# A recurrence feeding two gated layers: in the last two batches the r·u·k sums come from natural rows on GpSimd and VectorE instead of from one-column products

## The chip, the cores and the metric

The kernel runs on one core of one Trainium2 chip. The metric is device time in microseconds (us) for one execution: 479.68 us, the median of 3 runs (478.99 to 479.83). The engines are named as the profile names them: PE is TensorE (PEld its weight loads), DVE is VectorE, ACT is ScalarE, POOL is GpSimd, and SP issues the transfers.

## The reference

```python
B, H, S, D = 4, 8, 768, 48
for t in range(S):                                     # attention
    cur = einsum('bhd,bhe->bhde', u[None] * k_t, v_t)
    y[:, :, t] = einsum('bhd,bhde->bhe', r_t, state + cur)
    state = w_t[..., None] * state + einsum('bhd,bhe->bhde', k_t, v_t)
x = y.transpose(0, 2, 1, 3).reshape(B, S, H * D)       # 384 wide
h = gelu_tanh(x @ w_in);  u, v = h[..., :512], h[..., 512:]     # first layer
v_n = (v - mean(v)) / sqrt(var(v) + 1e-6) * g_ln
v_s = einsum('ts,bsd->btd', w_sg, v_n) + b_sg
x = x + (u * v_s) @ w_out                              # w_out 512 x 384
gate = sigmoid(causal convolution of x with 5 taps)    # second layer
out = (gate * (x @ w_val)) @ w_o2
```

The part that the change concerns is the own-token term of the recurrence: `r_t · (u * k_t)` is one number per token and head, the sum over d of r·u·k, and it scales v_t. Call these numbers the sums of r·u·k: 8 heads by 768 tokens in each of 4 batches.

## The kernel before

**The attention in units.** The recurrence is done in chunks of 64 tokens. A *unit* is one batch, one segment of 256 tokens and one pair of heads, so there are 12 units in a batch (3 segments by 4 pairs) and 48 in all. One packed transfer, `pk`, brings w, k and r of a unit with channels on the partitions; `sv` brings v for the chunks, and `v` (tile `vt`) brings natural rows of v: tokens on the partitions, all 384 columns.

A unit goes through these steps, whose letters the code uses. F and E (lines 396 and 401) are scans on DVE that make products of decays; L (`r_part`, 405) multiplies r by E on POOL; K (`k_part`) multiplies k by F; q (`ruk`, 412) multiplies r by k into the tile `q`. On PE, t (`turn`) transposes the decayed k; s (`scores`) makes the chunk's scores; B (`kv`, 447) makes each chunk's sum of k times v, and then the sums of r·u·k; C (`tokens`, 500) makes the outputs. After t, ACT copies the transposes (`kx`); after s, DVE masks the scores (`mx`). After B, ACT starts the chunk states (`gx`) and DVE chains them (step a, `states`, 491: tile `st`), then z saves the carry. `own_v` (o, 462) has ACT copy the sums out of PSUM (tile `rsw`) and POOL multiply natural v by them into the tile `y`. `y_out` (y, 515) adds what C made to `y`.

**The sums of r·u·k before.** In `kv`, lines 456 to 460, eight products of a unit take a 64 x 64 block of q as weights and one column of u (in the tile `misc`) as the moving operand: `pe.matmul(out=o[hh][half[c2], RS + j:RS + j + 1], lhsT=q[half[hh], ...], rhs=u_col[half[hh], ...])`. Each is a *one-column product*. A float32 product on 64 x 64 blocks stands in the trace as two records, so a unit has 16 of them.

**Visits.** All PE work of a unit's neighbours shares one two-bank PSUM tile, `p`. A *visit* is C of unit n-2, B of unit n-1, and t and s of unit n (`VISIT`, line 537). The results must be read out before the next visit writes there.

**The dense work.** Everything else on PE is dense: `xT` turns y, `hv` and `ups` are the two halves of x @ w_in, `vps` mixes tokens with w_sg, `c` is the first output product, `val` and `o` belong to the second layer. Weights and activations are split in high and low parts, so that each product takes three passes. The attention of batch b + 1 runs beside the dense work of batch b (`phase`, line 830); the last batch's dense work runs alone.

**What sets the order.** The program first records every instruction under a word with a number (`kx3`, `vs17`), and then emits them in the order of the list `SCHEDULE` (lines 55 to 193, used at 934). Each engine takes its own instructions in that order, one queue per engine; the transfers stand in SP's queue in the same way.

Of the kernel before, what the change touches and what calls it, by code (L numbers as in the profile page):

```python
# [15 lines left out]
F32 = mybir.dt.float32  # L16
# [7 lines left out]
DM = H * D  # L24
# [31 lines left out]
ini0 pk0 zp0 wps0 ld1 pk1 sv9 pk2 wl0 nat0 ld0 F0 wl1 sv2 K0 E0 wl2 sv0 F1 L0 pk3 E1 wm0 wm4 F2 L1  # L56
t0 wm4 wl3 q1 s0 K1 wm1 kx1 q0 dec0 wm2 wl4 K2 t1 sv3 dec0 s1 wm3 E2 sg0 kx0 dec1 dec0 B0 sv6 L2 mx1
mx0 dec0 ox0 wm9 ow0 gx2 wm9 wm10 pk4 dec1 gx1 kx2 wm10 dec0 sv1 ow2 t2 gx0 wm5 dec1 ow3 wm6 dec2 q2
pk5 B1 a0 dec1 wm7 dec2 s2 a0 dec3 wl5 F3 C0 kx3 dec2 kx4 E3 dec4 dec2 L3 gx4 ox1 gx3 z0 ox2 mx2 yc1
gx5 dec3 ow1 K3 wm15 ow7 yx0 wm15 dec3 B2 dec4 wm8 pk10 dec3 pk6 wm16 a1 dec4 sv4 wm11 a1 sg1 q3  # L60
dec3 pk9 C1 nat1 dec1 spl9 sv11 wm12 F4 spl0 yc0 wm16 spl9 t3 s3 dec4 dec5 wm13 dec2 gx6 wm14 gx7
ow5 wm17 E4 kx5 wm18 gx8 spl1 dec5 L4 z1 mx3 ox3 yx1 ow8 wm21 dec4 yd0 yc2 wm21 spl4 wm22 dec5 wm19
wl6 ow9 K4 ow6 mx5 sg2 ow4 mx4 B3 spl2 dec5 pk7 spl3 pk8 a2 wm22 spl1 spl10 wl7 sv7 a2 C2 ow10 F5
wl8 s4 sv10 t4 K5 z2 yx2 wm20 pk11 gx9 dec5 U4 wm27 yc3 wm27 ox4 ox5 wm23 gx11 spl10 gx10 wl9 wm28
ow13 wm24 kx6 a3 ow11 q4 ow15 E5 kx7 B4 spl5 spl2 dec6 L5 wm28 spl11 mx6 t5 yx4 wm25 yx3 a3 yd1 dec6
s5 C3 q5 spl0 wm29 ox6 yc4 ow12 wm29 spl11 yd2 wm30 gx12 ow16 wm30 ow14 F6 wm26 spl3 gx14 nat2 U5
gx13 sv5 dec7 yx5 xT0 a4 ow18 yc5 xTo0 dec7 yd3 xT1 a4 spl5 z3 xTo0 hv0 xTo1 mx7 kx8 dec7 K6 hv0 sg5
xTo1 dec6 hv0 a4 E6 hv1 ln0 F7 L6 C4 z4 dec6 B5 K7 s6 mx8 t6 E7 wm31 yc6 gx17 hv1 gx16 q6 U7 L7 yc7
ln0 kx9 wm31 mx10 hv1 ow17 dec7 gx15 U6 wm32 a5 kx10 dec7 ox7 ow19 B6 ox8 a5 ow23 q7 ln1 wm32 a5 F8
C5 s7 K8 yx7 yx6 t7 mx9 E8 yd4 wm33 gx18 gx19 wm33 wm34 kx11 z5 a6 ln0 gx20 wm34 a6 ow22 B7 ow21 L8  # L70
a6 ox9 ow20 spl8 t8 spl4 yx8 U8 s8 ln1 mx11 ow26 C6 z6 ow27 F9 ln1 sg4 gx22 sv8 gx21 kx12 a7 yc9 sg3
yc8 E9 gx23 wm35 yd5 kx13 ow25 a7 wm35 ox11 wm36 K9 ow24 q8 ow29 wm36 ox10 ln1 L9 t9 mx12 B8 yx10
ow31 a7 spl7 C7 dec6 pk12 ow28 s9 F10 ow30 gx24 yc10 ln0 K10 yx9 yx11 wm37 E10 ox12 spl6 xT2 wm37
wm38 ln0 xTo2 L10 wm38 ow34 xTo2 hv2 gx25 kx14 a8 U10 spl8 mx14 hv2 mx13 gx26 z7 ow32 a8 hv2 yd6 U9
a8 yc11 ow35 F11 yd7 wm39 ln2 t10 q9 B9 E11 s10 C8 q11 pk13 L11 sv13 xT3 ow33 ln2 q10 kx16 K11 wm39
gx29 wm40 yx13 gx27 gx28 wm40 a9 ox14 ln2 yc12 t11 xTo3 mx15 a9 spl7 kx15 xTo3 ox13 ow39 B10 ow38
yx12 mx16 ln2 s11 a9 C9 q12 U11 F12 hv3 ox15 gx30 ow42 a10 yc13 kx17 wm41 q13 gx31 wm41 K12 yc14
wm42 gx32 a10 wm42 ow37 E12 ow40 B11 ow43 a10 ow36 L12 mx17 C10 F13 yd8 hv3 pk14 ox17 gx33 ow45 nat3
gx34 a11 hv3 ox16 ow41 K13 ld2 ow44 a11 yc16 E13 gx35 yc15 ln3 a11 L13 yx16 yx15 yx14 t12 ln2 pk15
wm43 yd9 wm43 ln1 s12 yd10 ow47 C11 kx18 ln3 F14 spl6 yc17 kx19 ow46 spl13 yx17 xT4 spl13 s13 yd11  # L80
xTo4 B12 mx19 spl12 ln3 xTo4 xT5 E14 t13 xTo5 hv4 spl12 L14 dec9 mx18 hv4 gx36 xTo5 gx37 dec8 a12
hv5 dec9 gx38 q15 ln3 hv4 dec8 dec9 kx20 a12 hv5 dec9 ln4 K14 u0 z12 dec8 hv5 dec9 dec8 wl10 u0 ox18
ln5 ln3 sv12 o12 u0 mx20 u1 dec8 B13 ln4 F15 wl11 ln4 dec10 vs0 spl15 dec10 q14 t14 ln4 dec10 C12
K15 pk16 dec10 spl14 spl15 s14 wl12 uo0 vs0 E15 wl13 gx39 nat4 u1 ln4 L15 sv14 vs0 mx21 dec11 yx18
vs1 dec10 dec11 kx21 u1 spl14 gx40 vs1 dec11 uo1 a13 dec11 vs0 gx41 ox19 yc18 a13 vs2 dec11 yd12 vs1
cw0 ln5 F16 dec12 ln5 vs1 spl16 z13 dec12 C13 ln5 spl16 B14 dec12 dec13 ln5 vs0 dec13 vs1 dec12
dec13 s15 dec12 t15 dec13 vs0 E16 vs1 vs2 dec13 L16 vso0 vs2 spl18 wl14 vso1 vs2 ix2 gx43 wl15 kx22
wl16 spl17 vs2 gate0 sv15 gx44 ix1 gate1 vs2 gate0 pk17 mx22 gate1 gate0 ix0 yc19 gx42 gate1 u2 vso2
dec14 o13 wo0 K16 u2 dec14 spl17 u3 a14 vs3 dec15 dec14 a14 ox20 u2 spl18 o14 yx19 vs3 dec16 dec15
yd13 U16 z14 dec16 B15 dec14 s16 dec16 C14 dec14 vs3 dec15 spl19 dec16 t16 spl19 vs3 gx47 yc20 dec16  # L90
ox21 vs3 sg6 F17 spl21 vs3 gx46 u3 uo2 q16 gx45 spl21 wo1 pk18 dec15 wo2 sv16 a15 sg9 u3 i0 K17
# [922 lines left out]
```

## Time and profile before

| | |
|---|---|
| median of 3 runs | 479.68 us |
| the profiled execution | 479.42 us, of which the span of the trace is 477.5 us |
| PE busy | 456.3 us, 96% |
| DVE busy | 390.9 us, 82% |
| ACT busy | 266.5 us, 56% |
| POOL busy | 141.8 us, 30% |
| transfers | 44.03 MB, mean 92 GB/s |

An engine's share of the span is a mean over stages that differ, so it is read stage by stage. Matmuls are pipelined and their ends are modelled; two neighbouring rows of a PE timeline can overlap, and what a group of matmuls costs PE is the distance from its start to the start of the next group.

### The profile page before, as it was taken

The numbers are of one execution on the slowest core, as the hardware profiler recorded it, in microseconds if no ns is written. First come the engines' busy times: TensorE is split into PE (matmuls) and PEld (weight loads), VectorE is DVE, ScalarE is ACT, GpSimd is POOL, SyncE is SP. The second block draws the span as 40 slices with busy tenths as digits, with TensorE's granted clock in tenths as the row PEclk, the third lists the DMA queues.
The fourth block names the chain that finished last, engine by engine and source line by source line (L and its number), as shares of the span: only waits on it lengthen the run. The fifth ranks groups of instructions, "written<-read, shape, count | busy, mean of one in ns | idle before, by whom it ended". The sixth has DMA issues, their size and how long they took to land.

```text
span 477.5 us, 14571 instructions
## 1 busy us (share of the span) xinstructions
PE 456.3 (96%) x5940; PEld 412.0 (86%) x5940; DVE 390.9 (82%) x956; ACT 266.5 (56%) x810; POOL 141.8 (30%) x209
## 2 busy tenths in 40 slices
PE   8877898999999999999999999999999999999996
PEld 4655676888989988999999988999999989999995
DVE  5999999999998788767999899677988894326783
ACT  1586998744745388523745398433534696224253
POOL 4227655343523322322126122330133313100200
PEclk9899999999999999999999999999999999999999
DMA  8986124644413411143134131133122100000002
GB/s 265 353 265 207 27 71 134 185 142 127 134 44 88 140 55 47 47 131 108 44 93 135 45 101 60 35 101 113 39 77 85 35 1 1 34 18 0 1 17 83
DMA packets 25218, 44.03 MB, mean 92 GB/s; under 512 B 2880, under 2 KB 16832, under 8 KB 25152
## 3 DMA queue, kind: packets, MB, share of 16 engines
q1 hardware_dynamic: 25152, 43.11, 28.7%
q8 instruction: 46, 0.75, 0.7%
q14 instruction: 20, 0.16, 0.1%
HBM read 38.39 MB, written 4.72 MB: 90 GB/s over the span
## 4 chain that ended last, share of the span: by engine, by line
PE 71%; DVE 12%; ACT 5%; DMA 3%; issue 2%; POOL 1%; SPq 1%; ACTq 0%
PE vps L939 18%; PE p L939 11%; PE c L939 9%; PE ups L939 8%; PE hv L939 8%; PE o L939 8%; PE val L939 7%; DVE spare L939 3%; ACT vg L939 1%; DMA bits<-in_w_o_dram 1%; DMA bits<-in_w_val_dram 1%; DVE st L939 1%; PE a L939 1%; DVE F L939 1%; DVE late L939 1%
## 5 line engine op out<-in xcount | busy, mean ns | idle before, releaser
L939 PE MATMUL vps<-wsg,vnt 128*128 128x384 f32 x576 | 116.7, 341 | 0.0
L939 PEld LDWEIGHTS vps<-wsg,vnt 128*128 128x128 f32 x576 | 99.9, 188 | 0.6
L939 PE MATMUL ups<-x,win 128*128 128x384 f32 x288 | 61.9, 342 | 1.7 <-DVE gl L939 1.1
L939 PE MATMUL c<-gl,late 128*128 128x384 f32 x288 | 60.4, 340 | 0.0
L939 PE MATMUL hv<-win,x 128*128 128x512 f32 x216 | 58.2, 404 | 0.9 <-DVE x L939 0.9
L939 POOL TENSOR_TENSOR L<-pk,E 128x256 f32<-128x256 f32 x38 | 27.4, 722 | 98.4 <-PE p L939 29.9
L939 ACT ACTIVATE st<-p,F 128x48 f32<-128x48 f32 x144 | 39.9, 305 | 24.7 <-PE p L939 23.8
L939 PEld LDWEIGHTS ups<-x,win 128*128 128x128 f32 x288 | 50.6, 188 | 3.2 <-DVE gl L939 1.4
L939 PEld LDWEIGHTS c<-gl,late 128*128 128x128 f32 x288 | 50.0, 188 | 1.4 <-DVE gl L939 0.3
L939 DVE SCALAR_TENSOR_TENSOR cvp<-x,cw_col,cvp 128x384 f32<-128x384 f32 x84 | 49.7, 615 | 1.1 <-ACT cvp L939 0.5
L939 DVE SCALAR_TENSOR_TENSOR st<-st,F 128x48 f32<-128x48 f32 x128 | 40.8, 319 | 11.2 <-ACT st L939 10.3
L939 PE MATMUL o<-late,ml 128*128 128x384 f32 x216 | 47.1, 345 | 0.0
L939 PEld LDWEIGHTS hv<-win,x 128*128 128x128 f32 x216 | 38.8, 189 | 8.8 <-DVE x L939 1.7
L939 PE MATMUL val<-x2hl,late 128*128 128x384 f32 x216 | 43.7, 340 | 0.7 <-DVE gl L939 0.6
L939 POOL TENSOR_TENSOR x<-x 128x384 f32<-128x384 f32 x24 | 25.9, 1091 | 46.4 <-DVE cvp L939 43.5
L939 PEld LDWEIGHTS o<-late,ml 128*128 128x128 f32 x216 | 37.8, 188 | 2.1 <-DVE ml L939 0.7
L939 PEld LDWEIGHTS val<-x2hl,late 128*128 128x128 f32 x216 | 37.6, 188 | 1.9 <-DVE gl L939 0.9
L939 POOL TENSOR_TENSOR y<-s,y 128x96 f32<-128x96 f32 x48 | 24.8, 520 | 47.7 <-ACT s L939 17.7
L939 DVE TENSOR_TENSOR_SCAN F<-pk,D1F 128x260 f32<-128x260 f32 x40 | 29.9, 748 | 4.0 <-DMA pk<-in_pk_dram 3.7
L939 POOL TENSOR_TENSOR y<-v,rsw 128x192 f32<-128x192 f32 x36 | 20.6, 573 | 42.0 <-ACT rsw L939 30.6
L939 PEld LDWEIGHTS <-D1F 128*128 128x128 bf16 x196 | 18.6, 104 | 15.6 <-issue 8.1
L939 DVE SCALAR_TENSOR_TENSOR vps<-vps,misc,b_bc 128x384 f32<-128x384 f32 x29 | 17.9, 620 | 16.9 <-PE vps L939 16.9
(129 smaller groups left out, 935.1 us busy)
## 6 DMA issues: line engine op xcount, KB each, us to landing
pk<-in_pk_dram SPq DMA_DIRECT2D x40, 386.5 KB, 3.3
v<-in_v_dram SPq DMA_DIRECT2D x12, 384.0 KB, 4.2
out_dram<-ot SPq DMA_DIRECT2D x24, 192.0 KB, 2.1
sv<-in_sv_dram SPq DMA_DIRECT2D x39, 96.0 KB, 3.1
bits<-in_w_in_dram SPq DMA_DIRECT2D x6, 512.0 KB, 7.4
room_l<-in_pk_dram SPq DMA_DIRECT2D x7, 386.5 KB, 6.3
bits<-in_w_o_dram SPq DMA_DIRECT2D x7, 384.0 KB, 5.6
spare<-in_w_sgT_dram SPq DMA_DIRECT2D x12, 192.0 KB, 2.8
```

The source lines that it names most:

```text
L939: f(*a, **k)
```

## The change

For the units of batches 2 and 3 (the third and the fourth), step q, the one-column products and `own_v` are left out. In their place comes `bonus`, once for each 128 tokens, 6 times a batch and 12 times in all. A transfer `rk` brings natural rows of r and k (128 tokens by twice 384 columns, 384 KB) into one buffer; POOL multiplies r by k, then by u (a tile `u_bc`, loaded once, with u on every partition); DVE sums each head's 48 columns (`tensor_reduce`, 384 columns to 8); POOL multiplies natural v by these sums into `y`. The next `rk` load must wait for the reduce, since there is one buffer. Batches 0 and 1 keep the one-column products; the tile that held q in three slots becomes the `rk` buffer, and batch 1 keeps its q there. A visit is recorded with s before t, and the whole list `SCHEDULE` is another one, 2846 entries in place of 2860, from the first load to the last store.

```diff
 SCHEDULE = """
-ini0 pk0 zp0 wps0 ld1 pk1 sv9 pk2 wl0 nat0 ld0 F0 wl1 sv2 K0 E0 wl2 sv0 F1 L0 pk3 E1 wm0 wm4 F2 L1
...
+gate18 u20 yx45 bon11 gate18 u20 gx122 gate19 mx48 wo55 uo20 a40 ix12 gate19 wo54 K42 wo56 L42 vs20
...
+    u_bc = const.tile([128, DM], F32, name="u_bc")
...
-             "D1E": (NW, 1, ""), "st": (SV, 3, ""), "cy": (D, NP, ""), "q": (SEG, 3, "")}
+             "D1E": (NW, 1, ""), "st": (SV, 3, ""), "cy": (D, NP, ""), "rk": (2 * DM, 1, "")}
...
+    def load_rk(i):
+        t = buf("rk", i, i // KS).rearrange("p (two f) -> p two f", two=2)
+        with step("rk"):
+            sp.dma_start(out=t, in_=rk_[i // KS, i % KS * 128:(i % KS + 1) * 128, :, :])
+
+    def bonus(b, i):
+        s, j = divmod(i, NT)
+        with step("bon"):
+            t = buf("rk", b * KS + i, b)
+            q = t[:, 0:DM]
+            pool.tensor_tensor(out=q, in0=q, in1=t[:, DM:2 * DM], op=ALU.mult)
+            pool.tensor_tensor(out=q, in0=q, in1=u_bc, op=ALU.mult)
+            hd = lambda a: a.rearrange("p (h d) -> p h d", d=D)
+            rs = r2.tile([128, H], F32, tag="rsn", name="rs")
+            dve.tensor_reduce(out=rs, in_=hd(q), op=ALU.add, axis=AX.X)
+            run_loads("rk", b * KS + i + 1)
+            if j == 0:
+                yt[b, s] = ry.tile([128, NT, DM], F32, tag="y", name="y")
+            pool.tensor_tensor(out=hd(yt[b, s][:, j, :]), in0=hd(vt[b, s][:, j, :]),
+                               in1=rs.unsqueeze(2).to_broadcast([128, H, D]), op=ALU.mult)
+
...
-        q = pkt[:, 0:SEG] if first else parts["q"][1][n % 3]
+        q = pkt[:, 0:SEG] if first else parts["rk"][1][0][:, n % 3 * SEG:(n % 3 + 1) * SEG]
...
-            for j in range(NT):
+            for j in range(NT if b < 2 else 0):
...
-    VISIT = "C2 B1 t0 s0 y2 U1 g1 a1 z1 k0 m0"
+    VISIT = "C2 B1 s0 t0 y2 U1 g1 a1 z1 k0 m0"
...
-    loads = {"pk": load_unit, "sv": load_sv}
-    loaded, user = {"pk": 0, "sv": 0}, {}
+    loads = {"pk": load_unit, "sv": load_sv, "rk": load_rk}
+    loaded, user = {"pk": 0, "sv": 0, "rk": 2 * KS}, {}
...
-                go(n, "q")
+                if b < 2:
+                    go(n, "q")
                 run_loads("pk", n + 1)
+                if p == 0 and b >= 2:
+                    for j in range(NT):
+                        bonus(b, s * NT + j)
...
+        if b == 2:
+            run_loads("rk", 0)
...
-            go(n - 1, "o")
+            if b < 2:
+                go(n - 1, "o")
...
+        small["U"] = (u_bc, u_.to_broadcast([128, DM]))
-        for c in "kMkvI s sk ks W kskvsk sks B":
+        for c in "kMkvI s sk ks W kskvsk sks BU":
```

PE, one visit of the last batch before. `p` is the shared PSUM tile; `ident,kh` is t, `v,kn` is B, `misc,q` are the one-column products, `L,kh` is s, and `st,L` with `sv,L` is C:

```order
L939 MATMUL p<-ident,kh_103 128x128 x2
L939 MATMUL ups<-x,win 128x384 x3
L939 MATMUL p<-v,kn_109 64x48 x8
L939 MATMUL p<-misc,q_120 64x1 x8
L939 MATMUL p<-L_98,kh_103 64x64 x8
L939 MATMUL p<-st_112,L_99 64x48 x4
L939 MATMUL p<-sv_101,L_99 64x48 x4
L939 MATMUL p<-st_112,L_99 64x48 x4
L939 MATMUL p<-sv_101,L_99 64x48 x4
L939 MATMUL vps<-wsg_256,vnt 128x384 x3
L939 MATMUL ups<-x,win 128x384 x6
```

One visit of the last batch in the changed kernel, with C first:

```order
L969 MATMUL ups<-x,win 128x384 x6
L969 MATMUL p<-st_113,L_100 64x48 x4
L969 MATMUL p<-sv_102,L_100 64x48 x4
L969 MATMUL p<-st_113,L_100 64x48 x4
L969 MATMUL p<-sv_102,L_100 64x48 x4
L969 MATMUL p<-v,kn_110 64x48 x8
L969 MATMUL p<-L_99,kh_104 64x64 x8
L969 MATMUL p<-ident,kh_104 128x128 x2
L969 MATMUL ups<-x,win 128x384 x6
```

The eight one-column products are gone, the visit stands in one piece, and t has moved from ahead of the visit, with three dense products in between, to its end.

POOL, a stretch at the end of the third batch before. `y<-v,rsw` is natural v times the sums of one unit, `L<-pk,E` is r times E of a unit to come, `y<-s2,y` is the end of `y_out`, and `rstd` belongs to the normalisation after `hv`:

```order
L939 TENSOR_TENSOR L2_100<-pk1_97,E0_108 128x256
L939 TENSOR_TENSOR y_483<-v_432,rsw_498 128x2x96
L939 TENSOR_TENSOR y_483<-v_432,rsw_505 128x2x96
L939 TENSOR_TENSOR y_483<-s2_497,y_483 128x96
L939 TENSOR_TENSOR L0_98<-pk0_96,E0_108 128x256
L939 TENSOR_TENSOR y_483<-s2_504,y_483 128x96
L939 TENSOR_TENSOR rstd_512<-rstd_512,misc_89 128x1
L939 TENSOR_TENSOR L1_99<-pk1_97,E0_108 128x256
L939 TENSOR_TENSOR y_483<-s2_507,y_483 128x96
```

POOL in the changed kernel, again at the end of the third batch; `rk0` is the one rk buffer:

```order
L969 TENSOR_TENSOR rk0_119<-rk0_119 128x384
L969 TENSOR_TENSOR L1_100<-pk1_98,E0_109 128x256
L969 TENSOR_TENSOR y_464<-v_433,rs_463 128x384
L969 TENSOR_TENSOR rk0_119<-rk0_119,u_bc_94 128x384
L969 TENSOR_TENSOR y_464<-v_433,rs_465 128x384
L969 TENSOR_TENSOR L2_101<-pk0_97,E0_109 128x256
L969 TENSOR_TENSOR y_431<-s2_462,y_431 128x96
L969 TENSOR_TENSOR L0_99<-pk1_98,E0_109 128x256
```

Products of 384 columns, on rk, by u, and of v, now stand between the products `L` of the units to come.

SP, the loads of the third batch before, then a stretch of the same batch after:

```order
L939 DMA pk_97<-in_pk_dram 128x773
L939 DMA sv_101<-in_sv_dram 128x192
L939 DMA pk_96<-in_pk_dram 128x773
L939 DMA out_dram<-ot 128x384 x2
L939 DMA sv_102<-in_sv_dram 128x192
L939 DMA pk_97<-in_pk_dram 128x773
L939 DMA sv_102<-in_sv_dram 128x192
```

```order
L969 DMA pk_98<-in_pk_dram 128x773
L969 DMA rk_119<-in_rk_dram 128x768 x2
L969 DMA sv_102<-in_sv_dram 128x192 x2
L969 DMA sv_103<-in_sv_dram 128x192
L969 DMA pk_97<-in_pk_dram 128x773
L969 DMA rk_119<-in_rk_dram 128x768
L969 DMA pk_98<-in_pk_dram 128x773
```

The rk loads stand in the one queue with the loads `pk`, `sv` and `v`; the second of the two rk rows cannot be issued before the reduce of the tile ahead of it.

## Rows read from the trace of the kernel before

**Rows 1.** The page: busy us (share) xinstructions; then forty equal slices in tenths.
```profile
PE 456.3 (96%) x5940; PEld 412.0 (86%) x5940; DVE 390.9 (82%) x956; ACT 266.5 (56%) x810; POOL 141.8 (30%) x209
...
PE   8877898999999999999999999999999999999996
...
PEclk9899999999999999999999999999999999999999
```

**Rows 2.** Stages: us; busy us (instructions) by engine; granted clock; transfer share; GB/s.
```profile
0.00:80.00 80.00, 65.97 (x1288) 47.91 (x1289) 72.57 (x192) 54.90 (x201) 39.52 (x53) 0.98 0.59 197
80.00:140.00 60.00, 56.84 (x728) 51.90 (x727) 58.76 (x154) 36.40 (x106) 23.41 (x30) 1.00 0.39 119
140.00:197.00 57.00, 57.00 (x810) 51.13 (x809) 48.31 (x128) 36.95 (x110) 16.07 (x28) 1.00 0.29 85
197.00:300.00 103.00, 102.99 (x1425) 95.87 (x1424) 89.47 (x218) 55.27 (x169) 30.68 (x48) 1.00 0.28 84
300.00:390.00 90.00, 90.00 (x1231) 84.33 (x1230) 72.50 (x174) 45.62 (x144) 23.17 (x39) 1.00 0.21 65
390.00:440.00 50.00, 49.93 (x280) 48.48 (x280) 22.97 (x46) 23.12 (x51) 6.03 (x9) 1.00 0.03 13
440.00:478.00 38.00, 33.56 (x189) 32.36 (x187) 26.34 (x51) 14.19 (x31) 2.96 (x3) 1.00 0.09 32
```

**Rows 3.** PE timeline, visit with t ahead: start us, us, operation, count.
```profile
238.55 1.72 PE L939 MATMUL val<-x2hl,late 128*128 128x384 f32 x9
240.11 0.38 PE L939 MATMUL p<-ident,kh 128*128 128x128 f32 x2
...
240.69 0.37 PE L939 MATMUL p<-misc,q 64*64 64x1 f32 x16
240.91 0.44 PE L939 MATMUL p<-L,kh 64*64 64x64 f32 x16
...
241.73 0.79 PE L939 MATMUL vps<-wsg,vnt 128*128 128x384 f32 x3
```

**Rows 4.** PE timeline, a visit with t at its end.
```profile
343.91 1.74 PE L939 MATMUL val<-x2hl,late 128*128 128x384 f32 x9
345.58 0.46 PE L939 MATMUL p<-L,kh 64*64 64x64 f32 x16
...
346.54 0.37 PE L939 MATMUL p<-misc,q 64*64 64x1 f32 x16
346.85 0.44 PE L939 MATMUL p<-ident,kh 128*128 128x128 f32 x2
347.04 1.29 PE L939 MATMUL vps<-wsg,vnt 128*128 128x384 f32 x6
```

**Rows 5.** Groups from 197 to 390 us: count, busy us, mean ns; idle ahead, releaser.
```profile
L939 POOL TENSOR_TENSOR x<-x 128x384 f32<-128x384 f32 x12 | 13.9, 1169 | 7.1 <-DVE cvp L939 4.2 <-DVE halo L939 2.9
L939 POOL TENSOR_TENSOR y<-v,rsw 128x192 f32<-128x192 f32 x23 | 13.3, 578 | 27.4 <-ACT rsw L939 16.0 <-DVE q L939 7.5 <-DVE vnt L939 3.9
...
L939 DVE TENSOR_TENSOR q<-pk 128x256 f32<-128x256 f32 x20 | 9.0, 451 | 0.0
...
L939 DVE TENSOR_TENSOR gl<-vps,gl 128x384 fp32r<-128x384 f32 x16 | 8.8, 552 | 2.7 <-ACT gl L939 2.6
```

**Rows 6.** DVE timeline, updates of step a in two units.
```profile
319.42 1.92 DVE L939 SCALAR_TENSOR_TENSOR st<-st,F 128x48 f32<-128x48 f32 x2 [0.81 <-ACT st L939]
...
350.60 0.26 DVE L939 SCALAR_TENSOR_TENSOR st<-st,F 128x48 f32<-128x48 f32 x1
```

**Rows 7.** POOL timeline beside the first of these.
```profile
319.29 1.99 POOL L939 TENSOR_TENSOR x<-x 128x384 f32<-128x384 f32 x2
```

**Rows 8.** POOL timeline ahead of the visit of rows 4.
```profile
341.98 0.68 POOL L939 TENSOR_TENSOR L<-pk,E 128x256 f32<-128x256 f32 x1 [5.12 <-issue]
```

**Rows 9.** Transfers: issues, KB each, median us from issue to landing.
```profile
pk<-in_pk_dram SPq DMA_DIRECT2D x40, 386.5 KB, 3.3
v<-in_v_dram SPq DMA_DIRECT2D x12, 384.0 KB, 4.2
```

More of the change, by code (lines that the diff above doesn't have):

```diff
@@ new lines @@
+mx41 vs15 U35 a33 outo7 vs15 gx100 bon7 outo7 yc38 vs14*2 L35 bon7 vs14 a33 pk37 wo37 a33 yx38 F36
+vs14*2 ha1 E36 ix11 B34 C33 vso14 s35 sv35 gate14 t35 ix10 vs15 outo8 K36 rk8 vs15 ix9 sv34 wo38
+mx42 nat9 vs15 gate14 L36 wo40 gx103 vso15 gx102 kx42 wo39 yd32 pk38 gate14 yd31 wo41 gate15 yc39
+xTo14 hv12 a34 bon8 gate15 a34 hv12 gx104 gate15 hv12 yx39 wo42 a34 yd33 ln12 F37 wo45 hv13 woo9 E37
+B35 C34 xTo14 xT15 wo43 xTo15 bon6 wo46 gx106 xTo15 woo9 bon8 hv13 x29 yx40 woo10 gx105 hv13 yc40
+a35 x210 yd34 a35 wo44 gx107 L37 woo9 ln13 s36 bon8 t36 a35 rk9 K37 hv14 i3 sv36 mx43 hv14 nat10
@@ new lines @@
+vs30 vso29 u31 ha3 gate29 wo86 cv19 gate29 u31 cv18 u31 cv18 vs30 uo31 gate29 vs30 cv18 vs31 cv19
+vs31*2 cv19 vs30 cv18 cv19 vs31 vs30 vs31 vso30 vs31 cv18 wo85 vso31 cv18 ix21 wo89 gate30 wo84
+gate31 ix23 wo88 gate30 wo87 gate30 ix22 val18 gate31 val18 gate31 val18 wo90 valo18 wo91 wo93 wo94
+woo21 wo92 i7 woo22 woo21 wo95 valo18 val19 woo22 woo23 x221 val20 woo22 cv21 val19 valo18 woo23
+val20 woo21 x223 val19 cv21 x222 val21 woo23 cv23 valo19 out54 cv21 val21 valo19 cv22 val20 valo19
+out55 cv22 val22 valo20 cv21 out56 val22 cv23 valo20 val22 valo20 out57 cv21 val21 cv23 cv21 out60
@@ L196 @@
+cv22 out58 cv23 outo18 out59 valo21 outo18 out62 cv22 valo21 val23 cv22 out61 cv23 val23 outo19
+valo21 val23 cv22 outo19 outo20 out64 valo22 cv23 out63 outo20 valo22 valo23 out65 valo22 out66
+valo23*2 out69 out68 outo21 out67 outo21 out70 out71 outo22*2 outo23*2"""
 RES = ALU.subtract
@@ L408, in k_part @@
         def k_part():
-            (pool if b == 0 else dve).tensor_tensor(
+            (dve if b > 0 else pool).tensor_tensor(
                 out=ch(kh), in0=ch(k), in1=f3[:, :, 1:W1], op=ALU.mult)
@@ L415, in turn @@
         def turn():
-            o = t["a"] = shared(n - 1)
+            o = shared(n - 1)
             for j in range(NT):
@@ L423, in scores @@
                     c = 2 * (hh ^ x) + c2
-                    pe.matmul(out=t["a"][hh][half[x], SC + c2 * C:SC + (c2 + 1) * C],
+                    pe.matmul(out=shared(n - 1)[hh][half[x], SC + c2 * C:SC + (c2 + 1) * C],
                               lhsT=kh[half[hh], c * C:(c + 1) * C],
@@ L428, in k_rows @@
         def k_rows():
-            for x, i in pair(t["a"]):
+            for x, i in pair(shared(n - 1)):
                 with step("kx"):
@@ L433, in causal @@
         def causal():
-            for x, i in pair(t["a"]):
+            for x, i in pair(shared(n - 1)):
                 sc = x[:, :, SC:SC + 2 * C].rearrange("p h (c t) -> p h c t", t=C)
@@ L512, in tokens @@
                                   rhs=(sv if i else st)[half[x], z],
-                                  start=(i == 0 or j == 1 or none), stop=(i == 1 or j == 1))
+                                  start=(i == 0 or none or j == 1), stop=(i == 1 or j == 1))
         def y_out():
@@ L558, in pair @@
         return [(x.unsqueeze(1), slice(i, i + 1)) for i, x in enumerate(o)]
-    loads = {"pk": load_unit, "sv": load_sv}
-    loaded, user = {"pk": 0, "sv": 0}, {}
+    loads = {"pk": load_unit, "sv": load_sv, "rk": load_rk}
+    loaded, user = {"pk": 0, "sv": 0, "rk": 2 * KS}, {}
     def run_loads(kind, done, most=NU):
-        while loaded[kind] < NU and most > 0:
+        while loaded[kind] < (B * KS if kind == "rk" else NU) and most > 0:
             n = loaded[kind]
-            t = buf(kind, n)
+            t = buf(kind, n, n // KS if kind == "rk" else None)
             if user.get(id(t), -1) >= done:
```

265 lines of the change are left out of this document (125 added, 140 removed).

## The prediction

> **What bounds the kernel now.** I read the busy shares and slices of the page first. PE is busy 96% of the span, and from the ninth of the forty slices on its digit is 9 in every slice but the last; the clock row says 9 from the third slice to the end [rows 1]. Then the stages, because a mean share hides where an engine waits. Up to 80 us PE is busy 65.97 of 80, from 80 to 140 us 56.84 of 60; there DVE is the full engine, 72.57 and 58.76. From 140 to 440 us PE is busy all the time, at a granted clock of 1.00, the upper of its two levels (2.4 GHz): 57.00, 102.99 of 103, 90.00 and 49.93 of 50. In the tail it is busy 33.56 of 38 [rows 2]. So there are two kernels one after the other: a start set by DVE and the loads, and a long stretch in which the time is the sum of what PE is given. The attention of batches 2 and 3, which the change touches, runs at about 197 to 390 us, wholly inside the second. What PE no longer does there comes off the time one for one, as long as nothing else becomes late; and DVE is busy 161.97 of those 193 us (89.47 + 72.50), so it isn't far behind PE.
>
> **What the change takes from PE.** In a visit's timeline the sixteen records of the one-column products start at 240.69 us and the next group, the scores, at 240.91: PE pays 0.22 us for them, although the row gives 0.37 to their overlapping durations [rows 3]. Where dense or 128-wide work comes next the same step is 0.31 us [rows 4], but then whichever 64-wide group is last pays the 0.09 more, so I count 0.22. 24 units by 0.22 are 5.28 us.
>
> The Trainium skill (TensorE: Matmul & The Clock Gate, section "Wait — 56ns, not 53.3ns?") states that starts of matmuls do not come closer than about 25 ns, however narrow they are. Sixteen records would then hold PE 0.40 us, an estimate from that page, and the change would give 9.6 us. The row says 14 ns a record here, so the trace does not bear the rule out for these products.
>
> **What the order does to PE.** A visit costs PE something for going over between 128-wide and 64-wide work, and t (the two transposes, 128 wide) can be beside the dense work or between. With t first, from the nine val products at 238.55 to the dense work at 241.73 is 3.18 us [rows 3]. With t at the end, the same nine products and the same groups take from 343.91 to 347.04, 3.13 us [rows 4]. By the order, 9 visits of batches 1 to 3 go from 64-wide work straight into t before, and 26 after. 17 by 0.05 are 0.85 us.
>
> **What it moves to other engines** (per unit or tile from the groups at 197 to 390 us).
> - DVE loses 24 products q at 0.451 us, 10.8 us [rows 5]. It gains 12 reduces of 384 columns, an operation that no row shows. From below it is bounded by nothing but zero, from above by twice the 384-column row gl, 1.10, as if it were held up. I take that row's 0.552, the same width: 6.6 us. DVE gets 4.2 us less to do; the bounds are 10.8 less and 2.4 more.
> - ACT loses 24 copies of four columns; it is off PE's path and I count nothing.
> - POOL loses 24 products of 192 columns at 0.578, 13.9 us, and gains 36 of 384 columns. The row of that width is x at 1.169 [rows 5], so 42.1 us; its two neighbours in the timeline took 1.99 together, 1.00 each [rows 7], which gives 36 from below. Net about 28 us. POOL is busy 53.85 us in this stretch (30.68 + 23.17) and would be at 82 of 193: far from full. Its cover is its idle time; it costs something only through what stands behind a product in its queue and through DVE.
> - The wait added to POOL: the first product of a tile waits for its rk load, and the load for the reduce before it. Behind it in POOL's queue stand `L`, which the scores need, `rstd`, which ACT waits for after hv, and the y of a visit, for which DVE waits. Before, `L` at 341.98 was done at 342.66 [rows 8], and the scores that use it began at 345.58 [rows 4]: 2.92 us of room. Two products ahead of it, 2.3 us, fit into that; a load that has just been issued does not, since one of nearly its size takes 3.3 us (pk) to 4.2 us (v) to land [rows 9]. The order puts most rk loads well ahead of their first product, so I cost this at nothing, with the upper bound under the rivals.
> - SP: 12 loads of 384 KB are added to a queue whose engines are busy 28% and 21% of the time there [rows 2]. Behind an rk load that waits for its reduce stand `sv` and `pk` of later units, loaded a visit or more ahead. Nothing, for the same reason.
> - DVE next to POOL. Two of the three updates of step a took 1.92 us together [rows 6] while POOL did two x products in 1.99 [rows 7]; 0.96 each, against 0.26 for such an update at 350.60, with POOL still [rows 6]. The extra POOL work lies beside exactly such operations.
>
> The Trainium skill (SBUF — State Buffer, section "Who interferes with whom") says why: a DVE instruction with two inputs in SBUF and a GpSimd instruction that reads SBUF exclude each other, and the later one waits for the whole of the other. The trace agrees: each update ended with a POOL product. By the rule it is a price of the change and not an accident of that place.
>
> So I put a price on it: 0.70 us (0.96 less 0.26) for an update held by one new product. From below it costs PE nothing: PE stayed at work all through that stretch [rows 2]. From above, all 36 products hold a DVE instruction that PE waits for, 25 us. I take two updates that reach PE, 1.4 us, near the lower end, since the row where it happened shows no wait of PE. All other cover named above stays as it is.
>
> **The start.** From 0 to 197 us no instruction is of another kind; but the list of the order is new there too. PE idles 14.03 + 3.16 = 17.2 us before 140 us [rows 2], and another order can have more or less of that. I see no sign, so zero, with a third of it, 5.7 us, as the bound either way.
>
> **The sum.** Against the profiled execution's own 479.42 us: 479.42 - 5.28 - 0.85 + 1.4 = 474.7. The median of the runs shown is 0.26 above that execution, so I forecast 474.9 for the median.
>
> **Rivals.**
> 1. *PE pays for the products' whole length.* If what stands behind a group of products can't use the time that they overlap, a unit gives back the 0.37 us of the row [rows 3] and not 0.22: 8.9 in place of 5.28, 471.3 us. Against it speaks that the scores start 0.22 after them. 7%. (The page on TensorE of the Trainium skill, named above, points the same way, with its 9.6.)
> 2. *The start decides.* For it: all the idle time of PE lies there, and every queue's order is changed. Against: the work is the same and DVE was full, which an order cannot make fuller. A third of the idle time more is 480.6, less is 469.2. 7% up, 6% down.
> 3. *The gain is given back in POOL's queue.* If the rk load is late at 4 or 5 of the 12 tiles, each sets `L` back by a landing of 3.3 us and two products of 2.3 less the room of 2.9, 2.7 us, of which PE has dense work for half: 6 us, 479.5. For it: one buffer, one queue of loads. Against: up to tens of schedule entries between load and product. 10%. That the products cost PE nothing because they ran beside something else, so that the change doesn't do what it says, gives 479 to 480 too; the starts speak against it. 3%.
> 4. *DVE, held by POOL, becomes the bound: slower.* The place is the loop B, gx, a, C of the units of batches 2 and 3. Each new POOL product that falls on a DVE operation with two inputs in SBUF (the scans, kh, the updates of a) holds it by 0.70 us, and C of the next visit waits on PE. From 9 such products of the 36 on (6.13 over 0.70) the gain is gone. At 12 it is 8.4 us, 479.68 - 6.13 + 8.4 = 482.0; at all 36, 498.7. For it: DVE is busy 84% there, and the two slow updates. Against: DVE loses 4.2 us of work, a visit's results are wanted only after several us of dense work, and PE went on in the stretch of the slow rows. 17%, at 482.0.
>
> **How the numbers follow.** The forecast has 50%, with a range of its own of 472 to 477.5. The runs shown lie within 0.18% of each other, so 0.2%, about 1 us, is what can be told from no change. Faster: 50 + 7 + 6 = 63%. The same: 10 + 3 = 13%. Slower: 7 + 17 = 24%. The range reaches down to 470.2, which takes in rival 1, and up to 482.5, which takes in rivals 2 (up) and 3 and the milder half of 4.
>
> **What would show it.** In the changed profile the one-column rows must halve, a visit of batch 2 or 3 must fall from 1.62 us (240.11 to 241.73) to 1.4 or less, and PE must stay full from 140 to 430 us. The stretch from the end of the start to the end must be 5 to 7 us shorter. POOL must be busy about 170 us (142 + 28), its rk products 1.0 to 1.2 us each, the reduce about 0.55 us. I am wrong if PE has idle time before its groups `p` in the second half with st, L or y as releaser (rivals 3 and 4), if POOL waits for rk loads by microseconds, or if the first 140 us differ by more than 2 us.

## The result: 474.27 us, 1% faster, and the profile after

| | before | after |
|---|---|---|
| median, same chip | 479.0 us (6 runs) | 474.27 us (6 runs, 473.64 to 477.47) |
| ratio to before | | 0.9906, 95% interval 0.9883 to 0.9928 |
| profiled execution, its span | 479.42, 477.5 us | 474.3, 472.5 us |
| PE busy | 456.3 us | 450.6 us |

The interval is 3.4 to 5.6 us of gain; 474.9 was forecast. The longest of the six runs had a granted clock of 0.988 over its span, the others 0.991 to 0.995. The page after answers to [rows 1]: busy us, share, instructions, and the slices of PE.

```profile
PE 450.6 (95%) x5556; PEld 406.3 (86%) x5556; DVE 385.0 (81%) x944; ACT 266.9 (56%) x786; POOL 162.3 (34%) x221
...
PE   6879899989999999999999999999999999999996
```

The stages after, with the columns of [rows 2] (us; busy us of PE, PEld, DVE, ACT, POOL; granted clock; transfer share; GB/s):

```profile
0.00:80.00 80.00, 66.26 (x1288) 49.28 (x1289) 68.79 (x192) 55.70 (x203) 39.21 (x53) 0.96 0.57 192
80.00:140.00 60.00, 55.93 (x721) 50.37 (x720) 58.51 (x155) 36.11 (x106) 21.61 (x29) 1.00 0.42 133
140.00:197.00 57.00, 56.67 (x777) 50.48 (x776) 49.10 (x121) 35.62 (x107) 25.59 (x37) 1.00 0.39 122
197.00:300.00 103.00, 103.00 (x1252) 95.71 (x1251) 90.66 (x215) 56.49 (x161) 44.02 (x58) 1.00 0.34 103
300.00:390.00 90.00, 90.00 (x1084) 83.83 (x1083) 71.85 (x174) 49.02 (x140) 24.33 (x36) 1.00 0.23 69
```

PE has 5.7 us less to do (456.3 less 450.6) and is still full from 197 to 390 us. It idles 17.8 us before 140 us (80 less 66.26, and 60 less 55.93) where it idled 17.2 before. I take the end of batch 1's last gelu of `hv` for the end of the start, 194.1 us before and 194.9 after; from there to the end of the span it is 283.4 us before and 277.6 after, 5.8 less (5 to 7 were forecast). So the time went where it was forecast: less PE work in a stretch that PE bounds, a start about as long as it was, and almost no new wait in between (0.3 us, from 140 to 197 us).

One visit of the third batch after, on PE (start us, us, operation, count), which answers to [rows 3] and [rows 4]:

```profile
240.16 0.68 PE L969 MATMUL ups<-x,win 128*128 128x384 f32 x3
240.77 0.33 PE L969 MATMUL p<-st,L 64*64 64x48 f32 x8
...
241.27 0.41 PE L969 MATMUL p<-v,kn 64*64 64x48 f32 x16
241.50 0.43 PE L969 MATMUL p<-L,kh 64*64 64x64 f32 x16
241.86 0.44 PE L969 MATMUL p<-ident,kh 128*128 128x128 f32 x2
242.06 0.77 PE L969 MATMUL ups<-x,win 128*128 128x384 f32 x3
```

From its first product to the dense work behind it the visit takes 1.29 us (240.77 to 242.06), against 1.62 before.

What POOL and DVE got, from 197 to 390 us (count, busy us, mean ns; idle ahead, what ended it), beside [rows 5], and the loads beside [rows 9]:

```profile
L969 POOL TENSOR_TENSOR rk<-rk 128x384 f32<-128x384 f32 x8 | 8.5, 1060 | 14.7 <-DMA rk<-in_rk_dram 14.7
L969 POOL TENSOR_TENSOR y<-v,rs 128x384 f32<-128x384 f32 x10 | 8.3, 833 | 14.1 <-PE a L969 9.1 <-DVE st L969 5.0
L969 POOL TENSOR_TENSOR rk<-rk,u_bc 128x384 f32<-128x384 f32 x8 | 8.3, 1036 | 0.2
...
L969 DVE TENSOR_REDUCE rs<-rk 128x8 f32<-128x384 f32 x8 | 4.3, 541 | 1.1 <-POOL rk L969 1.1
```

```profile
rk<-in_rk_dram SPq DMA_DIRECT2D x12, 384.0 KB, 3.3
```

The reduce takes 0.54 us (0.55 was forecast), the rk products 1.04 and 1.06 (1.0 to 1.2). I had counted 1.17 for each of the three products; the rk ones took about 1.05 and the product of v 0.83, so POOL stands at 162 us and not at 170. POOL does wait for rk loads, 14.7 us in this stretch, and nobody on PE's path notices.

### The profile page after: what moved, and what is told of

It is laid out like the page before. It is cut to its first block, busy times and chain, and to the rows that moved or that the text cites. A ratio compares the mean times of both kernels' runs of the same rounds, so it can differ in the third digit from the quotient of the medians.

```text
span 472.5 us, 13805 instructions
## 1 busy us (share of the span) xinstructions
PE 450.6 (95%) x5556; PEld 406.3 (86%) x5556; DVE 385.0 (81%) x944; ACT 266.9 (56%) x786; POOL 162.3 (34%) x221
## 4 chain that ended last, share of the span: by engine, by line
PE 77%; DVE 9%; ACT 5%; issue 1%; DMA 1%; SPq 0%; ACTq 0%; DVEq 0%
PE vps L969 19%; PE p L969 13%; PE hv L969 10%; PE c L969 9%; PE ups L969 9%; PE o L969 8%; PE val L969 7%; PE a L969 2%; DVE cvp L969 1%; DVE st L969 1%; ACT st L969 1%; ACT vg L969 1%; DVE y L969 1%; DVE F L969 1%; DVE vps L969 1%
## 5 line engine op out<-in xcount | busy, mean ns | idle before, releaser
L969 PE MATMUL vps<-wsg,vnt 128*128 128x384 f32 x576 | 115.5, 339 | 1.4 <-DVE gt L969 0.7
L969 PE MATMUL hv<-win,x 128*128 128x512 f32 x216 | 59.3, 405 | 0.3 <-ACT x L969 0.3
L969 DVE SCALAR_TENSOR_TENSOR st<-st,F 128x48 f32<-128x48 f32 x128 | 39.3, 307 | 14.0 <-ACT st L969 13.0
L969 ACT ACTIVATE gl<-vps 128x384 fp32r<-128x384 f32 x29 | 14.3, 493 | 33.8 <-DVE vps L969 20.1
L969 POOL TENSOR_TENSOR y<-s,y 128x96 f32<-128x96 f32 x48 | 22.2, 469 | 32.2 <-DVE y L969 17.1
L969 DVE TENSOR_TENSOR_SCAN F<-pk,D1F 128x260 f32<-128x260 f32 x40 | 28.9, 722 | 4.5 <-DMA pk<-in_pk_dram 4.3
L969 POOL TENSOR_TENSOR rstd<-rstd,misc 128x1 f32<-128x1 f32 x24 | 15.6, 650 | 46.0 <-DVE rstd L969 32.3
L969 ACT ACTIVATE ut<-ups 128x384 f32<-128x384 f32 x32 | 15.7, 490 | 25.5 <-PE ups L969 20.6
```

Of the source, the lines that this page charges most:

```text
L969: f(*a, **k)
```

## The experiments

Each ratio is to the kernel before on the same chip, with its 95% interval. Runs are set against the changed kernel by the difference of two such ratios (0.9906 is the changed kernel's), of about 479.5 us; the changed kernel itself was timed once, and not again beside each experiment. Unless a title says otherwise, an edit is made to the changed kernel.

**1. The one-column products put back, once and twice.** 192 of them, the eight of each unit of batches 2 and 3, with L as weights.

```diff
-            for j in range(NT if b < 2 else 0):
+            w1 = q if b < 2 else L[:, 0, :]
+            for j in range(NT):               # twice: range(NT if b < 2 else 2 * NT), and blocks 2 * (j % NT) + c2
...
-                        pe.matmul(out=o[hh][half[c2], RS + j:RS + j + 1], lhsT=q[half[hh], c * C:(c + 1) * C],
+                        pe.matmul(out=o[hh][half[c2], RS + j:RS + j + 1], lhsT=w1[half[hh], c * C:(c + 1) * C],
```

> The changed kernel with the eight one-column products of each unit of batches 2 and 3 put back on PE; their weights are blocks of L, so that no product q is needed, and nobody reads the result. Only PE work is added, 24 times 16 records. If PE pays the distance between starts (0.22 us a unit), the time rises by 5.3 us, from 474.3 to 479.6. If PE pays the whole length of the row (0.37 us a unit), it rises by 8.9 us to 483.2. If the products ran in time that PE had anyway, it stays at 474.3.

> As the run with the products put back, but every product twice, 24 times 32 records. By the distance between starts 10.6 us more than the changed kernel, 484.9; by the whole length 17.8 more, 492; if there is room beside other work, the second dose costs less or more than the first, else the same.

Once: 480.6 us, 1.0017 (0.9999 to 1.0035), 5.3 us above the changed kernel, give or take 1.4. Twice: 485.4 us, 1.0123 (1.0089 to 1.0158), 10.4 us above, give or take 2. The same visit in the profile of the first:

```profile
240.72 0.33 PE L970 MATMUL p<-st,L 64*64 64x48 f32 x8
...
241.22 0.41 PE L970 MATMUL p<-v,kn 64*64 64x48 f32 x16
241.45 0.37 PE L970 MATMUL p<-misc,L 64*64 64x1 f32 x16
241.67 0.44 PE L970 MATMUL p<-L,kh 64*64 64x64 f32 x16
242.04 0.44 PE L970 MATMUL p<-ident,kh 128*128 128x128 f32 x2
242.24 0.77 PE L970 MATMUL ups<-x,win 128*128 128x384 f32 x3
```

The products start at 241.45 and the scores at 241.67: 0.22 us, and the visit is 1.52 us against 1.29. Both doses cost the distance between starts (5.3 and 10.6), not the length of the row (8.9 and 17.8). The traces put it in the stretch where the products stand: from batch 1's last gelu of `hv` to the end of the span it is 282.6 us with one dose and 287.5 with two, against 277.6.

**2. The products left out of the kernel before, in its own order.**

```diff
-            for j in range(NT):
+            for j in range(NT if b < 2 else 0):
...
-                    act.activation(out=rs[:, i], in_=x[:, :, RS:RS + NT], func=AF.Copy)
+                    act.activation(out=rs[:, i], in_=x[:, :, (0 if b > 1 else RS):(0 if b > 1 else RS) + NT], func=AF.Copy)
```

> The kernel before, in its own order, without the one-column products of batches 2 and 3 and with nothing in their place: ACT copies four other columns of the same PSUM tile, so every wait, q, and the POOL products stay (own-token sums of these batches are wrong numbers). If the gain is PE work taken away, this alone gives 5.3 us, 479.0 to 473.7, as much as the whole change or more. If the new order is what gains, it stays at 479.0 and the rest of the change must carry the 4.7.

476.67 us, 0.9940 (0.9924 to 0.9956): 2.9 us less and not 5.3. PE is no longer quite full there:

```profile
197.00:300.00 103.00, 102.29 (x1238) 93.77 (x1236) 90.42 (x220) 56.39 (x172) 30.61 (x47) 1.00 0.28 83
300.00:390.00 90.00, 89.61 (x1080) 83.41 (x1080) 74.19 (x176) 47.12 (x148) 23.45 (x39) 1.00 0.21 64
```

The forecast took it that what PE no longer does comes off one for one. In the old order a part of it becomes waiting, 1.1 us in these two rows, and PE's busy time falls by only 2.5 us (456.3 to 453.8). The start isn't where the rest went: from batch 1's last gelu of `hv` to the end it is 280.7 us, 2.7 less than before. Summed from start to start, from 170 us to the end of the attention, the 64-wide groups and the transposes take 4.9 us less and the dense groups between them, waits included, 1.8 us more. Why dense groups without a wait are longer there I didn't find.

**3. The changed kernel without the new work.** Neither rk loads, products nor reduces; y is C's part plus natural v.

```diff
-                    dve.tensor_tensor(out=y, in0=z, in1=y, op=ALU.add)
+                    dve.tensor_tensor(out=y, in0=z, in1=y if b < 2 else g, op=ALU.add)   # g: natural v
...
-                    for j in range(NT):
-                        bonus(b, s * NT + j)
+                    yt[b, s] = ry.tile([128, NT, DM], F32, tag="y", name="y")
...
-        if b == 2:
-            run_loads("rk", 0)
```

> The changed kernel without bonus in batches 2 and 3 (no rk loads, no POOL products by k, u and v, no reduce; y takes C's output plus natural v, so the own-token term of these batches is left out of the computation). It shows what the new POOL, DVE and DMA work costs the changed kernel. By my forecast 1.4 us or less: 472.9 to 474.3. By the rival that DVE is held by POOL it would gain clearly more, 3 us or more.

475.68 us, 0.9915 (0.9897 to 0.9933): no faster than with it (0.4 us more, give or take 1.4), so the 1.4 us that I had allowed lie just outside what the runs leave open, and rival 4's 3 us or more are out. The 35 us of POOL work that the bonus adds (162.3 less 126.9 busy) cost PE nothing that can be measured. DVE's busy time falls by 6.7 us without it, of which the twelve reduces are 6.5; the updates `st` are 27 ns shorter on the mean (293 against 320 ns), so some are held.

**4. t moved between the other groups, in 36 visits.** One of them in the list:

```diff
-gate20 C40 xTo18 gate20 B41 L43 cv12 s42 x213 sv42 t42
+gate20 C40 xTo18 gate20 B41 L43 cv12 t42 s42 x213 sv42
```

> The changed kernel with the two transposes t of all 36 visits of batches 1 to 3 moved between the other groups of the visit, so that PE goes from 64-wide work to 128-wide and back once more in each. From the starts in the traces (0.15 us into t, 0.20 out of it into 64-wide work, against 0.03 out of t into dense work) this is about 0.3 us a visit where t stood at the end: 36 visits give up to 10.8 us, less for batch 1 where PE has room; 480 to 485. If the place of t costs nothing, so that my 0.85 us for the order was no gain, it stays at 474.3.

In this list t stands between 64-wide groups in 32 of the 36 visits, where it did in one; in the other four it has dense work ahead of it and 64-wide work behind. One visit of the last batch:

```profile
312.90 0.26 PE L974 MATMUL p<-st,L 64*64 64x48 f32 x2
...
313.40 0.42 PE L974 MATMUL p<-L,kh 64*64 64x64 f32 x14
313.75 0.44 PE L974 MATMUL p<-ident,kh 128*128 128x128 f32 x2
314.12 0.45 PE L974 MATMUL p<-v,kn 64*64 64x48 f32 x16
314.50 0.80 PE L974 MATMUL ups<-x,win 128*128 128x384 f32 x3
```

483.53 us, 1.0069 (1.0045 to 1.0092), 7.8 us more than the changed kernel, give or take 1.6, with no other work: 0.25 us for each of the 31 visits that got t between. The rows show where: from t to the next group is 0.37 us here (313.75 to 314.12) and 0.20 in the changed kernel's visit above, where dense work follows; and the last 64-wide group now pays the way to dense work, 0.38 (314.12 to 314.50) for B, which took 0.23 there. So the place of t can be worth as much as the eight products of a unit. PE's busy time grows too, from 450.6 to 459.9 us: the price stands in the distances between groups. The Trainium skill (TensorEngine Tiling (Array Packing), section "Key Properties") states that a change between tiling modes drains TensorE; the direction agrees, and the page gives no size.

**5. The bonus in the kernel before's order,** set into the old list by hand, q and own_v of batches 2 and 3 out.

```diff
-... L23 t23 q24 vs7 ix4 F24 ... cv3 val3 ox30 x25 cv4 o24 hv10 xTo11 ...
+... L23 t23 bon1 bon1 vs7 ix4 F24 ... cv3 val3 x25 cv4 bon0 bon1 hv10 xTo11 ...
```

> The bonus of batches 2 and 3 set by hand into the order of the kernel before: its list with q, the products and own_v of these batches taken out, and the rk loads and bonus pieces put where q and own_v stood (q of batch 1 in a tile of its own, four buffers for the small sums). No other entry moves. If the gain is the PE work of the products, this gains most of it: 474 to 476. If it needs the new order, it stays at 479 or is slower, with waits of POOL or PE at the new places.

487.45 us, 1.0135 (1.0108 to 1.0162): 6.5 us *slower* than before.

```profile
140.00:197.00 57.00, 54.34 (x761) 48.16 (x762) 49.02 (x121) 34.22 (x104) 24.46 (x36) 1.00 0.36 108
197.00:300.00 103.00, 98.95 (x1216) 90.28 (x1214) 88.12 (x204) 53.27 (x154) 37.19 (x51) 1.00 0.33 100
```

PE idles 2.7 and 4.1 us in stretches where it had no idle time. 3.0 us of its waits name the tile L, which DVE masks and POOL fills; two more, of 0.9 us each, name cy and st, on DVE:

```profile
PE p L975 <- DVE L L975: 1.5, 2, 1.2
PE p L975 <- POOL L L975: 1.5, 1, 1.5
```

One list set by hand is not the best one, and no run shows how far another would get; but it shows that the same work without room for it costs more than leaving the products out gives.

**6. Twice as much GpSimd work, in four forms.** First the product by u done three times, 24 products more (25.2 us of POOL).

```diff
-            pool.tensor_tensor(out=q, in0=q, in1=u_bc, op=ALU.mult)
+            for _ in range(3):
+                pool.tensor_tensor(out=q, in0=q, in1=u_bc, op=ALU.mult)
```

> The changed kernel with the product by u done three times in each of the 12 tiles (so the sums are those of r, k and u to the third power): 24 more POOL products of 384 columns, some 26 us of POOL work and of collisions with DVE. If POOL's work is covered, as forecast, under 1.5 us more: up to 475.8. If each product holds a DVE instruction that PE waits for, 24 times 0.7 us are 17 us: 491. If POOL's queue delays L, something between, with PE waiting ahead of the scores.

490.49 us, 1.0219 (1.0189 to 1.0249), 15 us more than the changed kernel, give or take 1.8. My forecast said less than 1.5. The reduce and the updates on DVE, from 140 us on, with what ended the idle time ahead of them, in the changed kernel and then here:

```profile
L969 DVE SCALAR_TENSOR_TENSOR st<-st,F 128x48 f32<-128x48 f32 x80 | 25.6, 320 | 10.5 <-ACT st L969 9.8
...
L969 DVE TENSOR_REDUCE rs<-rk 128x8 f32<-128x384 f32 x12 | 6.5, 540 | 2.0 <-POOL rk L969 2.0
```

```profile
L976 DVE SCALAR_TENSOR_TENSOR st<-st,F 128x48 f32<-128x48 f32 x79 | 27.2, 344 | 10.2 <-ACT st L976 9.6
...
L976 DVE TENSOR_REDUCE rs<-rk 128x8 f32<-128x384 f32 x12 | 6.6, 548 | 12.7 <-POOL rk L976 12.7
```

DVE stands 12.7 us at the reduce, and what PE wants next from DVE stands behind it in the queue; in the changed kernel it is 2.0 us. PE idles 11.2 us from 140 to 440 us, where it idled 0.3. The updates are held only a little more (344 ns, 320 in the changed kernel). This led to two theories: DVE *waits* at the reduce, or DVE is *held* by POOL's reads. Three runs tell them apart: the same work with the reduce later and two rk buffers; the 24 products on a tile that nobody reads, so that the reduce needn't wait; and 24 fills in their place, which read nothing.

```diff
 # reduce later: two rk buffers, and in the list
-bon5 ... C27 bon5 nat8 s29 E30 B28 sv28 t29 outo5 wo25 gx84 rk6 L30 U29 yx33 u12 sv29 a28 gx86 ix8 gate10
+bon5 ... C27 nat8 s29 E30 B28 sv28 t29 outo5 wo25 gx84 rk6 L30 U29 yx33 u12 sv29 a28 gx86 ix8 bon5 gate10
 # free reduce
+            for _ in range(2):
+                pool.tensor_tensor(out=spare_q, in0=u_bc, in1=u_bc, op=ALU.mult)
 # fill
+                pool.memset(spare_q, 0.0)
```

> The changed kernel with the product by u done three times (the 24 additional GpSimd products of the run that took 15 us more, sums of r*u*k with u to the third power), but with two rk buffers and each reduce 18 entries later in the list, about 3 us. Theory A: those 15 us came from VectorE standing at the reduce until GpSimd had finished (12.7 us of waits there, 2.0 in the changed kernel), with everything behind it in VectorE's queue; the later reduce finds its data ready: 475 to 480. Theory B: they came from GpSimd holding VectorE's operations with two SBUF inputs, or from L, y and rstd late in GpSimd's queue; both are as before: 486 to 492.

> The changed kernel with 24 additional GpSimd products of the same width at the same places of GpSimd's queue as in that run, but into a tile that nobody reads (u times u), so that the reduce need not wait for them; the output is the full one. Theory A (VectorE standing at the reduce): 474.5 to 479, and waits of the reduce for GpSimd back at about 2 us. Theory B (GpSimd's products hold VectorE, or what is behind them in GpSimd's queue is late): as there, 486 to 492.

> The changed kernel with 24 additional GpSimd instructions at the places of the run with 24 products of u by u, but each a fill of 800 columns with zero, which reads nothing from SBUF and should take about as long (a fill of 260 columns takes 0.32 us, a product there 0.85). The output is the full one. In that run 3.6 us more and 5.0 us more of VectorE busy time were measured than in the changed kernel. Theory H (GpSimd products that read SBUF hold VectorE's operations with two SBUF inputs): VectorE back at 384 to 387 us busy, and 474 to 476 us. Theory Q (what stands behind the additional instructions in GpSimd's queue is late): 477 to 479 us, with VectorE at 385 or 390 alike.

| 24 instructions more on POOL | ratio (interval) | us above the changed kernel | DVE busy us | DVE waits at the reduce | PE idle, 140 to 440 us |
|---|---|---|---|---|---|
| none (changed kernel) | 0.9906 (0.9883 to 0.9928) | 0 | 385.0 | 2.0 | 0.3 |
| products ahead of the reduce | 1.0219 (1.0189 to 1.0249) | 15.0 | 388.6 | 12.7 | 11.2 |
| the same, reduce later | 1.0096 (1.0068 to 1.0124) | 9.1 | 394.9 | 0.1 | 5.3 |
| products beside the reduce | 0.9981 (0.9966 to 0.9995) | 3.6 | 390.0 | 2.0 | 3.8 |
| fills beside the reduce | 0.9944 (0.9918 to 0.9970) | 1.8 | 384.2 | 2.0 | 0.5 |

The three columns on the right are of one profiled execution each. The updates `st` in the last three, in this order, the last with POOL's fill ahead of them:

```profile
L978 DVE SCALAR_TENSOR_TENSOR st<-st,F 128x48 f32<-128x48 f32 x79 | 29.1, 368 | 10.1 <-ACT st L978 9.0 <-ACT s L978 0.5
```

```profile
L979 DVE SCALAR_TENSOR_TENSOR st<-st,F 128x48 f32<-128x48 f32 x79 | 28.1, 356 | 10.4 <-ACT st L979 9.9
```

```profile
L979 POOL MEMSET spare_q<- 128x800 f32 x24 | 18.4, 768 | 0.7
...
L979 DVE SCALAR_TENSOR_TENSOR st<-st,F 128x48 f32<-128x48 f32 x79 | 24.9, 315 | 10.8 <-ACT st L979 10.4
```

Both theories hold, in parts. Freed from the wait, the products cost 3.6 us in place of 15 (they are also shorter, 0.85 us against 1.05). The run with the later reduce refutes my expectation for it (475 to 480): the waits at the reduce are gone and 9.1 us stay, beside 9.9 us more busy time of DVE. Its reduces fall elsewhere, and DVE's operations with two SBUF inputs are longer than in the others: the scans F take 828 ns on the mean, 712 in the changed kernel, and the updates 368. So 6 to 11 of the 15 us go when the wait goes, and how the 15 split is not settled more closely.

Holding is real by itself: with products beside it DVE is busy 5.0 us longer than in the changed kernel, with fills it isn't, and the updates are back at 315 ns. It reaches PE, which idles 3.8 us beside the products and 0.5 beside the fills, as good as the changed kernel's 0.3. The medians alone don't tell the two apart: the fills' 1.8 us lies between, and its interval overlaps with both neighbours. The Trainium skill (SBUF — State Buffer, section "Who interferes with whom") states that a DVE instruction with two SBUF inputs contends with a GpSimd instruction that reads SBUF and not with one that only writes; the products and the fills agree, with 390.0 and 384.2 us.

**7. The bonus in batch 1 too,** first as the old steps stand, then with two rk buffers, the first loads 90 entries earlier and the reduces later.

```diff
-            for j in range(NT if b < 2 else 0):
+            for j in range(NT if b < 1 else 0):
-                if p == 0 and b >= 2:
+                if p == 0 and b >= 1:
 # then, in the list
-q9 ld3 ... q11 rk0 ... s11 bon0 bon0 bon0 rk1 kx16
+q9 ld3 rk0 rk1 ... q11 ... s11 bon0 bon0 kx16 ... yx13 bon0 rk2
```

> The changed kernel with the bonus in batch 1 too, put by hand into its order: 12 more units lose their one-column products, 6 more tiles gain rk work. If PE is the bound from 140 us on, where about two thirds of these visits lie, it gains up to 12 times 0.22, 2.6 us: 471.7 to 473.5. If the first 140 us, where DVE and the loads set the pace, don't take it, or the hand-set places make POOL wait for its loads, 474.3 or more.

489.59 us, 1.0202 (1.0171 to 1.0233), 14 us more than the changed kernel. The start shows a full chain of what I had called rival 3. POOL, then DVE, from 65 us on:

```profile
69.40 0.99 POOL L974 TENSOR_TENSOR rk<-rk 128x384 f32<-128x384 f32 x1 [2.67 <-DMA rk<-in_rk_dram]
70.47 0.99 POOL L974 TENSOR_TENSOR rk<-rk,u_bc 128x384 f32<-128x384 f32 x1
```

```profile
71.49 0.55 DVE L974 TENSOR_REDUCE rs<-rk 128x8 f32<-128x384 f32 x1 [4.47 <-POOL rk L974]
71.96 0.26 DVE L974 SCALAR_TENSOR_TENSOR st<-st,F 128x48 f32<-128x48 f32 x1
```

The load is late by 2.67 us, POOL needs 2 us more, DVE stands at the reduce for 4.47, and the update `st` that is queued behind it, which needs nothing of all this, comes about 4.5 us late. PE waits 4.8 us there.

> The sums from natural rows in batches 1 to 3, as in the run that took 14 us more than the changed kernel, but with two rk buffers, the first two rk loads issued some 90 entries earlier, and the reduces of batch 1 18 entries later. There the first rk load landed 2.7 us after GpSimd wanted it, and VectorE stood at the first reduce for 4.5 us and TensorE for 4.8. Theory A (late loads and VectorE standing at the reduce are the loss): 472 to 477, at best 2.6 us (12 units of 0.22) below the changed kernel. Theory B (the start has no room for more GpSimd and VectorE work in any place): 481 to 488.

485.01 us, 1.0111 (1.0079 to 1.0142): still 9.8 us more than the changed kernel, in the range of theory B (481 to 488). The late load, with the reduce behind it, was about a third of the loss. In the start DVE is the full engine, and this order by hand has no room for more; whether another one would, no run here tells. The granted clock differs too: up to 80 us and from 80 to 140 us it is 0.94 and 0.97 in the first of these profiles and 0.94 and 0.91 in the second, against 0.96 and 1.00 in the changed kernel's. In the first it fell to the lower of its two levels at 71 us, late in PE's 4.8 us wait. So a part of each loss is the clock's, and I didn't separate it. It isn't the whole: with a clock of 0.995 over the span the second took 482.53 us, and the changed kernel 473.64 and 475.01.

No version tried beats the changed kernel.

## Why the prediction was right, step by step

- *The bound.* That PE's work from 140 to 440 us is the time held: PE is busy 5.7 us less (forecast 6.1), the stretch behind the start is 5.8 us shorter, and the medians differ by 4.7 us.
- *24 units by 0.22 us.* Right in size and mechanism: 5.3 us for one dose, 10.4 for two, and the same distance in the row. This also settles rival 1 (0.37 a unit): it would have been 8.9 and 17.8. The Trainium skill (TensorE: Matmul & The Clock Gate, section "Wait — 56ns, not 53.3ns?") states a floor of about 25 ns from start to start, by which I estimated 9.6 us; neither the trace (14 ns a record, for these products on 64 x 64 blocks) nor the 5.3 us of one dose agrees.
- *0.85 us for the place of t.* Not resolved by itself. With the products put back, what is left of the change is 1.0017 of before, 0.8 us more (0 less to 1.7 more), and the forecast's two other terms make +0.55. The two traces have it the other way behind the start, 282.6 us against 283.4, with one execution of each. That the place of t has a price was right; run 4 puts the price of the worst place at 0.25 us a visit.
- *1.4 us for two held updates.* Too much in this order: without all of the new work it is no faster. Holding took place (320 against 293 ns a `st`), but PE didn't wait for it.
- *The sum.* That it came within 0.6 us is in part luck. Without the 1.4 the forecast would have been a gain of 6.1 us, and 3.4 to 5.6 were measured. If the new work costs nothing and the products are worth 5.3, the new order by itself gave nothing in the medians where I had put 0.85: two small terms, each off or unresolved, that cancel.
- *"All other cover stays as it is."* True of this order, and luckier than the text says. I costed the rk load and POOL's queue by POOL's idle time and by the 2.92 us of room of `L`. Neither was the nearest edge. The nearest that the runs found is the reduce: an instruction in DVE's queue that waits for POOL, with all of DVE's work behind it. My part on the added wait listed what stands behind the first product on POOL, and not what stands behind the reduce on DVE. Its room is what the order gives it; 24 products more used it up at once (15 us, 6 to 11 of them by the wait).
- *Rival 4,* slower by holding: it didn't come, but it is no phantom: with 24 products more DVE is busy 4 to 10 us longer, and beside the reduce PE idles 3.8 us for it.
- *Rival 3,* a late load: POOL waited 18.7 us for rk loads from 140 us on, which I had put down as a sign of being wrong. It wasn't: PE had nothing behind those waits. In run 7 such a wait cost PE 4.8 us, as the reduce stood behind it.
- *The start.* Zero was right within a microsecond (0.8 us later at its end).

What the forecast didn't say is that its first step needs the new order. In the old one, leaving out the products gives 2.9 us and the whole replacement loses 6.5.

## What to carry to other kernels

On the engine that bounds the time, price a group of narrow products by the distance from its start to the next start, and look for what it costs to change shape around it, which can be as much again. When work is moved to idle engines, don't count their idle time: list each instruction that waits across engines, and ask what is queued behind *it*. And judge a change of work together with its order: the same work was worth -4.7 us in one order and +6.5 in another, which was set by hand.

## What the runs showed of the hardware that I had not expected

- A pair of transposes between 64-wide groups and not at the end costs 0.25 us a visit (7.8 us, 31 visits), without any wait that the profile names: PE is busy 299.65 of the 300 us from 140 us on.
- A fill of 800 columns on POOL (0.77 us) leaves DVE's two-input updates alone (315 ns), where a product that reads SBUF lengthens them (356 ns on the mean).
- A product of 384 columns on POOL takes 1.04 to 1.08 us on the mean with rk and another input of full width (x, before, 1.17), and 0.83 to 0.86 us with one tile as both inputs or with eight sums repeated.
